# Reordering the three passes of the down products in a two-layer MoE kernel

## The chip, the cores and the metric

One Trainium2 chip, one core. The metric is the device time of one execution in microseconds; lower is better. The chip's engines are called as the profile calls them: PE (TensorE matmuls), PEld (TensorE weight loads), DVE (VectorE), ACT (ScalarE), POOL (GpSimd), SP (SyncE, which issues the transfers here).

## The reference

Attention with a memory term comes first, then two feed-forward layers over 2304 tokens (d_model 512, d_ff 2048). The two layers, cut to what matters here:

```python
def _moe_ref(x, w_in, w_out):
    h = x @ w_in
    g = np.maximum(0.01 * h, h)
    return (g @ w_out).astype(np.float32)

def _moe2_ref(x, w_in, w_out):
    h = x @ w_in
    g = h - np.tanh(h)
    return (g @ w_out).astype(np.float32)
```

`x @ w_in` is called up in the kernel, `g @ w_out` down.

## The kernel before

Each operand of the up and down products is split into a high part, rounded for one-pass matmuls, and a low part, the rest. A product is then three passes: high by high, high by low and low by high. The weights of both layers lie in SBUF as pairs `[high | low]` of 512 columns each; the activations as `gh` and `gl` (`xs[:, 0]` and `xs[:, 1]` for the input).

Tokens are cut into 9 blocks of 256, d_ff into 8 pairs of 128 columns (index `p`, with `s` for the two halves of a pair). For one block and one pair, an item below, the work is: 24 up matmuls (line 846) of 256 columns into one PSUM tile; the activation, which makes `g`; its high part `gh`, then its low part `gl`, which is `g - gh` and so comes after `gh`; and the down products, summed over all `p` in PSUM.

In layer 1 the down product has the weights as its stationary operand and `gh` or `gl` as its moving one: 24 matmuls of 256 columns (line 948) into `dn0` and `dn1`, each of which holds two of the four 128-row slices `m`. In layer 2 the activation is stationary and the weights move: 12 matmuls of 512 columns (line 1114) into two full tiles `dn[0]` and `dn[1]`, one for each half `t` of the tokens. The up matmuls of both layers, in `three()` (lines 843 to 849), run their three passes directly behind each other, with the same stationary tile in the first two.

The order of the work is set in two ways. Attention and layer 1 are put in order by a planner (`Schedule`, lines 86 to 221), which runs when the kernel is built: each piece of work has a cost in ns, what it reads and writes, and a priority. The planner goes forward in time; whenever an engine is free it gives it the first piece in order of priority whose inputs are there. Pieces of attention go ahead of pieces of layer 1 on PE (priority 0 against `MOE_PE` = 1), and the downs of item `p` (priority `2 * seq + 3`) go behind the ups of item `p+1` (`2 * (seq + 1)`). A down piece is two matmuls, at a cost of 240; an up piece is three, at 354. The result is one fixed order for each engine; on the chip an engine that waits for an input does not go on to what is behind it.

Layer 2 is ordered by hand (lines 1134 to 1152). Step `i` issues the ups of item `i`, its activation chain `act2` (inside which `act2_end` makes `gh` on ACT and `gl` on POOL for item `i-1`), and the downs of item `i - LAG2`, with `LAG2 = 2`. After the downs of a block's last item, `end2` copies `dn[0]` and then `dn[1]` out on ACT and stores them.

Of the kernel before, what the change touches and what calls it, by code (L numbers as in the profile page):

```python
# [9 lines left out]
F32 = mybir.dt.float32  # L10
# [213 lines left out]
MOE_PE = 1  # L224
# [18 lines left out]
def kernel(  # L243
# [14 lines left out]
    nc = tc.nc  # L258
    B, H, D, S = qkt.shape[0], qkt.shape[1], qkt.shape[2], qkt.shape[3] // 2
    DM, DFF = w1_in.shape  # L260
    KT = DM // 128
# [64 lines left out]
    for i in range(2):  # L326
        p = slice(64 * i, 64 * i + 64)
# [3 lines left out]
    wt = [[None] * NF for m in range(2)]  # L331
# [38 lines left out]
    p1 = ExitStack()  # L370
# [5 lines left out]
    dn_p = p1.enter_context(tc.tile_pool(name="dn", bufs=1, space=PSUM))  # L376
# [5 lines left out]
    sc = Schedule(RINGS)  # L382
    x_h = {}
    w_h = [[sc.new(None) for f in range(NF)] for m in range(2)]
# [468 lines left out]
    def layer1(n, p0, p1):  # L853

        kind, b = blocks[n]
        sop = lambda *a, **kw: sc.op(*a, prio=(-1, n), **kw)
        again = p0 > 0
        if again:

            halves = [sc.new("e0"), sc.new("e1")]  # L860

            def load_half(e, i):
                halves[i].tile = att.tile([128, 2, 256], F32, name=f"e{i}", bufs=1)
                nc.sync.dma_start(out=halves[i].tile, in_=xsv[n][:, 2 * i:2 * i + 2])

            for i in range(2):
                sop([("sp", 600)], lambda e, i=i: load_half(e, i), reads=[xv_h[n]], alloc=[halves[i]], lat=2600)
        elif kind == "R":
            x = sc.new("x")

            def load_x(e):
                x.tile = x_p.tile([128, KT, 256], F32, name="x")
                nc.sync.dma_start(out=x.tile, in_=x8s)

            sop([("sp", 600)], load_x, reads=[x8_h], alloc=[x], lat=2600)
        else:
            x = x_h[kind, b]
            if p1 < NP:

                def save_x(e):  # L880
                    nc.sync.dma_start(out=xsv[n], in_=x.tile)

                sop([("sp", 600)], save_x, reads=[x], writes=[xv_h[n]], lat=2600)
        xs = sc.new("xs")

        def x_half(i):
            return halves[i].tile if again else x.tile[:, 2 * i:2 * i + 2]

        def x_hi(e, i):
            if xs.tile is None:  # L890
                xs.tile = xs_p.tile([128, 2, KT, 256], F32R, name="xs")
            copy(e, xs.tile[:, 0, 2 * i:2 * i + 2], x_half(i))

        def x_lo(e, i):
            low(e, xs.tile[:, 1, 2 * i:2 * i + 2], x_half(i), xs.tile.bitcast(F32)[:, 0, 2 * i:2 * i + 2])

        for i in range(2):
            xi = halves[i] if again else x
            sop([("act", ACT(512)), ("dve", DVE(256))], lambda e, i=i: x_hi(e, i), reads=[xi] + [xs] * i,
                writes=[xs], alloc=[] if i else [xs])  # L900
            lo = sop([("dve", DVE(512))], lambda e, i=i: x_lo(e, i), reads=[xi, xs], writes=[xs])
            if again:
                att_ops.append(lo)
        dn = [sc.new("dn0"), sc.new("dn1")]
        last = None
        for p in range(p0, p1):
            seq = seqs[0]
            seqs[0] += 1
            ps = sc.new("up")

            def first_up(e, f, ps=ps):
                ps.tile = up_p.tile([128, 2, 256], F32, name="up")
                f()

            for s, kt, three in up_mms(lambda: xs.tile, lambda ps=ps: ps.tile, p):
                one = s == 0 and kt == 0
                sc.op(
                    [("pe", 354)], (lambda e, f=three, ff=first_up: ff(e, f)) if one else three,
                    reads=[xs, w_h[0][2 * p + s]] + ([] if one else [ps]), writes=[ps],
                    alloc=[ps] if one else [], prio=(MOE_PE, 2 * seq), order=one)  # L920
            g, gl, gh = sc.new("g"), sc.new("gl"), sc.new("gh")

            def leak(e, ps=ps, g=g):
                g.tile = g_p.tile([128, 512], F32, name="g")
                nc.scalar.activation(  # L925
                    out=g.tile, in_=ps.tile.rearrange("p a b -> p (a b)"), func=AF.Prelu, alpha=0.01)

            def g_hi(e, g=g, gh=gh):
                gh.tile = g_p.tile([128, 512], F32R, name="gh", bufs=RINGS["gh"])
                copy(e, gh.tile, g.tile)  # L930

            def g_lo(e, g=g, gh=gh, gl=gl):
                gl.tile = g_p.tile([128, 512], F32R, name="gl", bufs=RINGS["gl"])
                low(e, gl.tile, g.tile, gh.tile.bitcast(F32))

            sop([("act", ACT(512, True))], leak, reads=[ps], alloc=[g])
            sop(copies(512), g_hi, reads=[g], alloc=[gh])
            last = sop(lows(512), g_lo, reads=[g, gh], alloc=[gl])
            for j, (wh, gg) in enumerate(((0, gh), (1, gh), (0, gl))):
                for s in range(2):  # L940
                    for mm in range(0, KT, 2):

                        def down(e, p=p, j=j, wh=wh, gg=gg, s=s, mm=mm):
                            if p == p0 and j == 0 and s == 0:
                                dn[mm // 2].tile = dn_p.tile([128, 2, 256], F32, name=f"dn{mm // 2}")
                            w = wt[1][2 * p + s]
                            for m in (mm, mm + 1):
                                nc.tensor.matmul(  # L948
                                    dn[m // 2].tile[:, m % 2, :],
                                    lhsT=w[:, wh * 512 + m * 128:wh * 512 + (m + 1) * 128],  # L950
                                    rhs=gg.tile[:, s * 256:(s + 1) * 256],
                                    start=(p == p0 and s == 0 and m % 2 == 0 and j == 0),
                                    stop=(p == p1 - 1 and s == 1 and j == 2), skip_group_check=True)

                        begin = p == p0 and j == 0 and s == 0
                        d = dn[mm // 2]
                        sc.op([("pe", 240)], down, reads=[gg, w_h[1][2 * p + s]] + ([] if begin else [d]),
                              writes=[d], alloc=[d] if begin else [], prio=(MOE_PE, 2 * seq + 3))
        for i in range(2):
            x2 = sc.new("g")  # L960
            half = slice(2 * i, 2 * i + 2)

            def part_load(e, x2=x2, half=half):
                x2.tile = g_p.tile([128, 2, 256], F32, name="g")
                nc.sync.dma_start(out=x2.tile, in_=xps[n][:, half, :])

            def x2_out(e, i=i, x2=x2):
                if p0 > 0:
                    nc.vector.tensor_tensor(out=x2.tile, in0=dn[i].tile, in1=x2.tile, op=ALU.add)
                else:  # L970
                    x2.tile = g_p.tile([128, 2, 256], F32, name="g")
                    copy(e, x2.tile, dn[i].tile)

            def x2_store(e, x2=x2, half=half):
                nc.sync.dma_start(out=(x2s if p1 == NP else xps)[n][:, half, :], in_=x2.tile)

            if p0 > 0:
                sop([("sp", 500)], part_load, reads=[xp_h[n][i]], alloc=[x2], after=[last], lat=2300)
                sop([("dve", DVE(512))], x2_out, reads=[dn[i], x2], writes=[x2], port=False)
            else:  # L980
                sop(copies(512, True), x2_out, reads=[dn[i]], alloc=[x2], port=False)
            sop([("sp", 500)], x2_store, reads=[x2], writes=[x2_h[n] if p1 == NP else xp_h[n][i]], lat=2300)
# [57 lines left out]
    for p in range(NP):  # L1040
        for m in range(2):
            for f in (2 * p, 2 * p + 1):
                t = sc.new("v2")
# [60 lines left out]
    def down2(n, p):  # L1104
        if p == 0:
            state["dn"] = [dn2_p.tile([128, 512], F32, name=f"dn{i}") for i in range(2)]
        dn = state["dn"]
        gh, gl = state.pop((n, p))
        for j, (g, wh) in enumerate(((gh, 0), (gh, 1), (gl, 0))):
            for s in range(2):  # L1110
                w = wt[1][2 * p + s]
                for t in range(2):
                    c0 = s * 256 + t * 128
                    nc.tensor.matmul(  # L1114
                        dn[t], lhsT=g[:, c0:c0 + 128], rhs=w[:, wh * 512:(wh + 1) * 512],
                        start=(p == 0 and s == 0 and j == 0), stop=(p == NP - 1 and s == 1 and j == 2))
                    yield "pe"
# [16 lines left out]
    for i in range(len(items) + LAG2):  # L1134
        if i < len(items):
            n, p = items[i]
# [60 lines left out]
```

## Time and profile before

| | |
|---|---|
| median of 3 runs | 1082.89 us (1082.38 to 1083.25) |
| the profiled execution, whole | 1082.97 us |
| its span, first to last instruction | 1080.9 us |
| PE matmul busy | 1046.0 us, 97% |
| DVE busy | 754.3 us, 70% |
| ACT busy | 637.5 us, 59% |
| POOL busy | 104.0 us, 10% |
| mean granted TensorE clock | 0.988 of full speed |

The span leaves out about 2 us that lie around it. A matmul's own duration in the trace (about 285 ns for 256 columns) includes its way through the array, which overlaps with the next one's; what a matmul costs in a stream is the distance between starts. Rows that merge several instructions give the start of the first and the time they cover; in the chain of work that ended last the covered time is cut so that nothing is counted twice, and dividing it by the count gives the cost of one.

### The profile page before, as it was taken

Reading aid. Unit: us, or ns where it says so; the run is one execution under the profiler, and the core shown is the slowest. Engines: PE = TensorE matmul, PEld = TensorE weight load, DVE = VectorE, ACT = ScalarE, POOL = GpSimd, SP = SyncE. Lnnn points to the kernel's source line nnn. Section 1 sums busy time; section 2 is a strip of 40 time slices with the busy share of each in tenths; the row PEclk is TensorE's granted clock in tenths of the full one; section 3 lists DMA queues with packets and bytes.
Section 4 is the critical chain, followed back from the end, with each engine's and each line's share of the span. In section 5 each row is a group of like instructions: output and inputs, shape, how many; then the busy total and the mean of one; then the engine's idle time right before and its main releaser. Section 6 shows DMA issues by size and latency. Waiting matters only on the chain.

```text
span 1080.9 us, 20416 instructions
## 1 busy us (share of the span) xinstructions
PE 1046.0 (97%) x7488; PEld 921.3 (85%) x7488; DVE 754.3 (70%) x2044; ACT 637.5 (59%) x1357; POOL 104.0 (10%) x107
## 2 busy tenths in 40 slices
PE   5799999999999999999999999999999999999997
PEld 3567798787678977979999999999999999999996
DVE  6999999878766577664222267867777676777764
ACT  6899876667564266462111134766666666666664
POOL 1000000000000000000000000222222222221221
PEclk8699999999999999999999999999999999999999
DMA  7867754556554354243100056010101101010000
GB/s 231 261 178 219 232 173 119 158 144 166 158 147 135 114 159 140 91 124 124 40 2 21 1 156 196 1 40 1 40 1 39 40 1 40 1 40 20 1 20 20
DMA packets 116404, 102.53 MB, mean 95 GB/s; under 512 B 63824, under 2 KB 92496, under 8 KB 116304
## 3 DMA queue, kind: packets, MB, share of 16 engines
q1 hardware_dynamic: 116304, 101.23, 31.4%
q8 instruction: 59, 0.97, 0.4%
q14 instruction: 41, 0.34, 0.1%
HBM read 78.65 MB, written 22.54 MB: 94 GB/s over the span
## 4 chain that ended last, share of the span: by engine, by line
PE 77%; DVE 9%; DMA 6%; ACT 5%; issue 2%; SPq 1%; ACTq 0%; DVEq 0%
PE up L846 33%; PE dn L1114 18%; PE dn L948 14%; PE s L701 3%; PE s L582 3%; PE o L723 3%; DMA cv<-in_moe_w_out_dram 2%; DVE e L608 1%; PE o L668 1%; DVE cv L792 1%; DVE cv L797 1%; PE s L587 1%; ACT e L628 1%; DVE w L410 1%; DMA rq<-in_q_dram 1%
## 5 line engine op out<-in xcount | busy, mean ns | idle before, releaser
L846 PE MATMUL up<-xs,w 128*128 128x256 f32 x3456 | 454.4, 285 | 3.8 <-ACT g L925 2.4
L846 PEld LDWEIGHTS up<-xs,w 128*128 128x128 f32 x3456 | 435.2, 191 | 17.4 <-issue 6.2
L948 PE MATMUL dn<-gh,w 128*128 128x256 f32 x1152 | 161.1, 287 | 0.5 <-DVE gh L399 0.5
L948 PEld LDWEIGHTS dn<-gh,w 128*128 128x128 f32 x1152 | 146.5, 192 | 4.8 <-issue 3.6
L1114 PE MATMUL dn<-w,gh 128*128 128x512 f32 x576 | 145.3, 394 | 1.3 <-ACT gh L1101 1.3
L1091 DVE SCALAR_TENSOR_TENSOR gf<-u,w 128x512 f32<-128x512 f32 x72 | 86.2, 1197 | 82.3 <-ACT w L1088 82.3
L410 POOL TENSOR_TENSOR gl<-gf,gh 128x512 fp32r<-128x512 f32 x72 | 93.4, 1297 | 507.9 <-ACT gh L1101 504.4
L925 ACT ACTIVATE g<-up 128x512 f32<-128x512 f32 x72 | 42.7, 592 | 136.5 <-PE up L846 131.3
L1114 PEld LDWEIGHTS dn<-w,gh 128*128 128x128 f32 x576 | 103.0, 188 | 21.2 <-ACT gh L1101 2.0
L1083 ACT ACTIVATE u<-up 128x512 f32<-128x512 f32 x72 | 43.1, 598 | 123.8 <-PE up L846 123.8
L628 ACT ACTIVATE e<-e,mx 128x128 f32<-128x128 f32 (+4 forms) x144 | 82.7, 576 | 12.2 <-DVE mx L608 9.1
L948 PE MATMUL dn<-gl,w 128*128 128x256 f32 x576 | 85.0, 286 | 0.0
L948 PEld LDWEIGHTS dn<-gl,w 128*128 128x128 f32 x576 | 75.3, 192 | 3.2 <-issue 3.1
L1114 PE MATMUL dn<-w,gl 128*128 128x512 f32 x288 | 77.3, 390 | 0.0
L399 DVE CAST gh<-g 128x512 fp32r<-128x512 f32 x32 | 13.6, 426 | 87.6 <-ACT g L925 87.6
L608 DVE CUSTOM_DVE_ANT_0 e<-s,mask 128x128 f32<-128x128 f32 (+4 forms) x144 | 63.6, 481 | 12.3 <-PE s L582 6.5
L701 PE MATMUL s<-identr,e 128*128 128x128 f32 x448 | 64.7, 286 | 7.1 <-ACT e L645 5.2
L397 ACT ACTIVATE pt<-s 128x320 f32<-128x320 f32 (+4 forms) x145 | 56.4, 433 | 18.4 <-PE s L689 10.9
L701 PEld LDWEIGHTS s<-identr,e 128*128 128x128 f32 x448 | 51.1, 145 | 16.7 <-ACT e L645 7.4
L1114 PEld LDWEIGHTS dn<-w,gl 128*128 128x128 f32 x288 | 54.1, 188 | 12.1
L582 PE MATMUL s<-qk 64*128 64x256 f32 (+3 forms) x256 | 53.7, 497 | 9.7 <-DMA qk<-in_qkt_dram 7.0
L1085 DVE SCALAR_TENSOR_TENSOR hu<-up,u 128x512 f32<-128x512 f32 x72 | 49.6, 689 | 16.6 <-ACT u L1083 16.5
(100 smaller groups left out, 1329.4 us busy)
## 6 DMA issues: line engine op xcount, KB each, us to landing
w<-in_moe_w_in_dram SPq DMA_DIRECT2D x16, 512.0 KB, 5.0
w<-in_moe_w_out_dram SPq DMA_DIRECT2D x16, 512.0 KB, 5.6
cv<-in_moe_w_in_dram SPq DMA_DIRECT2D x32, 256.0 KB, 2.8
vs<-cv SPq DMA_DIRECT2D x64, 128.0 KB, 1.9
cv<-in_moe_w_out_dram SPq DMA_DIRECT2D x32, 256.0 KB, 2.9
v<-vs SPq DMA_DIRECT2D x32, 256.0 KB, 3.6
qk<-in_qkt_dram SPq DMA_DIRECT2D x16, 448.0 KB, 3.8
v<-in_v_dram SPq DMA_DIRECT2D x16, 320.0 KB, 3.4
```

The lines of the kernel that those rows point to most:

```text
L397: nc.scalar.activation(out=out, in_=in_, func=AF.Copy)
L410: (nc.vector if e == "dve" else nc.gpsimd).tensor_tensor(out=out, in0=in_, in1=high, op=ALU.subtract)
L582: nc.tensor.matmul(ss[j].tile[:, c0:c0 + nn], lhsT=qk.tile[p, a:a + 128], rhs=qk.tile[p, kc:kc + nn], start=True, stop=True)
L608: nc.vector.tensor_tensor_reduce(out=out, in0=in0, in1=in1, scale=-scale, scalar=mx.tile[:, 0:1] if t == 4 and j else BIG, op0=ALU.add, op ...
L628: nc.scalar.activation(out=x, in_=x, func=AF.Exp, scale=-1.0, bias=mx.tile[:, k:k + 1], accum_out=sm.tile[:, j:j + 1])
L701: nc.tensor.transpose(ss[j].tile[:, a:a + 128], x, ident)
L846: nc.tensor.matmul(ps()[:, s, :], lhsT=w[:, wh * 512 + kt * 128:wh * 512 + (kt + 1) * 128], rhs=xs()[:, xh, kt, :], start=(kt == 0 and j = ...
L948: nc.tensor.matmul(dn[m // 2].tile[:, m % 2, :], lhsT=w[:, wh * 512 + m * 128:wh * 512 + (m + 1) * 128], rhs=gg.tile[:, s * 256:(s + 1) * ...
L1083: nc.scalar.activation(out=u, in_=h, func=AF.Square)
L1085: nc.vector.scalar_tensor_tensor(out=hu, in0=h, scalar=c4, in1=u, op0=ALU.mult, op1=ALU.mult)
L1091: nc.vector.scalar_tensor_tensor(out=g, in0=u, scalar=lin, in1=w, op0=ALU.mult, op1=ALU.add)
L1114: nc.tensor.matmul(dn[t], lhsT=g[:, c0:c0 + 128], rhs=w[:, wh * 512:(wh + 1) * 512], start=(p == 0 and s == 0 and j == 0), stop=(p == NP - ...
```

## The change

In layer 1 the pieces of a down product become eight pieces of three matmuls, one for each half `s` and slice `m`; each runs the passes (high weights, `gh`), (high weights, `gl`), (low weights, `gh`) directly behind each other, costs 354 in the plan and reads both `gh` and `gl`. Before they were twelve pieces of two, which went through all of one pass before the next, and read `gh` or `gl`. In layer 2 the loop over the passes becomes the innermost: for each `s` and `t` the order is (`gh`, high weights), (`gh`, low weights), (`gl`, high weights). The number of matmuls is the same in both layers.

```diff
-            for j, (wh, gg) in enumerate(((0, gh), (1, gh), (0, gl))):
-                for s in range(2):
-                    for mm in range(0, KT, 2):
-
-                        def down(e, p=p, j=j, wh=wh, gg=gg, s=s, mm=mm):
-                            if p == p0 and j == 0 and s == 0:
-                                dn[mm // 2].tile = dn_p.tile([128, 2, 256], F32, name=f"dn{mm // 2}")
-                            w = wt[1][2 * p + s]
-                            for m in (mm, mm + 1):
-                                nc.tensor.matmul(
...
-                        sc.op([("pe", 240)], down, reads=[gg, w_h[1][2 * p + s]] + ([] if begin else [d]),
-                              writes=[d], alloc=[d] if begin else [], prio=(MOE_PE, 2 * seq + 3))
+            for s in range(2):
+                for m in range(KT):
+
+                    def down(e, p=p, gh=gh, gl=gl, s=s, m=m):
+                        if p == p0 and s == 0 and m % 2 == 0:
+                            dn[m // 2].tile = dn_p.tile([128, 2, 256], F32, name=f"dn{m // 2}")
+                        w = wt[1][2 * p + s]
+                        for j, (wh, gg) in enumerate(((0, gh), (0, gl), (1, gh))):
+                            nc.tensor.matmul(
...
+                    begin = p == p0 and s == 0 and m % 2 == 0
+                    d = dn[m // 2]
+                    sc.op([("pe", 354)], down, reads=[gh, gl, w_h[1][2 * p + s]] + ([] if begin else [d]),
+                          writes=[d], alloc=[d] if begin else [], prio=(MOE_PE, 2 * seq + 3))
...
-        for j, (g, wh) in enumerate(((gh, 0), (gh, 1), (gl, 0))):
-            for s in range(2):
-                w = wt[1][2 * p + s]
-                for t in range(2):
-                    c0 = s * 256 + t * 128
+        for s in range(2):
+            w = wt[1][2 * p + s]
+            for t in range(2):
+                c0 = s * 256 + t * 128
+                for j, (g, wh) in enumerate(((gh, 0), (gh, 1), (gl, 0))):
                     nc.tensor.matmul(
```

## Rows read from the trace of the kernel before

**Rows 1.** The page: busy time of PE, and the clock granted to it in 40 slices

```profile
PE 1046.0 (97%) x7488; PEld 921.3 (85%) x7488; DVE 754.3 (70%) x2044; ACT 637.5 (59%) x1357; POOL 104.0 (10%) x107
...
PEclk8699999999999999999999999999999999999999
```

**Rows 2.** Busy time in stretches: stretch, its length, then each engine, clock, DMA

```profile
0.00:60.00 60.00, 41.66 (x212) 28.18 (x213) 50.04 (x241) 45.53 (x135) 3.29 (x13) 0.80 0.80 238
60.00:500.00 440.00, 430.38 (x3297) 356.90 (x3297) 348.64 (x1321) 283.66 (x704) 7.28 (x22) 1.00 0.53 156
500.00:667.00 167.00, 167.00 (x1394) 167.00 (x1394) 62.11 (x112) 34.83 (x60) 0.00 (x0) 1.00 0.19 58
667.00:1075.00 408.00, 406.65 (x2592) 369.24 (x2590) 293.54 (x373) 272.36 (x458) 93.38 (x72) 1.00 0.07 24
```

**Rows 3.** The chain that ended last: start us, us, what; clean streams

```profile
358.76 2.88 PE up L846 x24
361.64 2.88 PE dn L948 x24
...
681.52 2.76 PE dn L1114 x12
```

**Rows 4.** The page's groups of instructions: the up matmuls and their weight loads

```profile
L846 PE MATMUL up<-xs,w 128*128 128x256 f32 x3456 | 454.4, 285 | 3.8 <-ACT g L925 2.4
L846 PEld LDWEIGHTS up<-xs,w 128*128 128x128 f32 x3456 | 435.2, 191 | 17.4 <-issue 6.2
```

**Rows 5.** Timeline of layer 2's first down product (start us, us, instructions)

```profile
674.93 0.63 ACT L1101 ACTIVATE gh<-gf 128x512 fp32r<-128x512 f32 x1 [0.61 <-DVE gf L1094]
...
675.61 2.12 PE L1114 MATMUL dn<-w,gh 128*128 128x512 f32 x8
675.64 1.29 POOL L410 TENSOR_TENSOR gl<-gf,gh 128x512 fp32r<-128x512 f32 x1 [203.39 <-ACT gh L1101]
...
677.57 1.07 PE L1114 MATMUL dn<-w,gl 128*128 128x512 f32 x4
```

**Rows 6.** Timeline of layer 2's last down product and the copies behind it

```profile
1071.58 0.63 ACT L1101 ACTIVATE gh<-gf 128x512 fp32r<-128x512 f32 x1 [2.47 <-DVE gf L1094]
1072.26 1.69 PEld L1114 LDWEIGHTS dn<-w,gh 128*128 128x128 f32 x8 [1.71 <-ACT gh L1101]
1072.26 2.12 PE L1114 MATMUL dn<-w,gh 128*128 128x512 f32 x8 [1.29 <-ACT gh L1101]
1072.28 1.29 POOL L410 TENSOR_TENSOR gl<-gf,gh 128x512 fp32r<-128x512 f32 x1 [3.51 <-ACT gh L1101]
...
1074.21 1.07 PE L1114 MATMUL dn<-w,gl 128*128 128x512 f32 x4
1075.09 1.09 ACT L1122 ACTIVATE ob<-dn 128x512 f32<-128x512 f32 x2 [2.88 <-PE dn L1114]
```

**Rows 7.** Timeline of layer 2 in its steady state

```profile
802.09 1.30 POOL L410 TENSOR_TENSOR gl<-gf,gh 128x512 fp32r<-128x512 f32 x1 [4.35 <-ACT gh L1101]
...
805.58 1.78 PE L1114 MATMUL dn<-w,gh 128*128 128x512 f32 x7
```

**Rows 8.** The instructions of line 948: durations in ns, first and last start

```profile
L948 PEld LDWEIGHTS dn<-gh,w x1152: 186/192/249, 60.2 to 665.6; 128*128 128x128 f32 x192
```

**Rows 9.** Timeline of layer 1 at two of its 72 down products

```profile
205.01 0.69 DVE L410 TENSOR_TENSOR gl<-g,gh 128x512 fp32r<-128x512 f32 x1 [0.39 <-ACT gh L397]
205.03 1.25 PEld L948 LDWEIGHTS dn<-gh,w 128*128 128x128 f32 x10 [0.25 <-ACT gh L397]
...
350.14 1.29 DVE L410 TENSOR_TENSOR gl<-g,gh 128x512 fp32r<-128x512 f32 x2
...
350.25 1.55 PE L948 MATMUL dn<-gh,w 128*128 128x256 f32 x11 [0.47 <-DVE gh L399]
```

More of the change, by code (lines that the diff above doesn't have):

```diff
@@ L938, in layer1 @@
             last = sop(lows(512), g_lo, reads=[g, gh], alloc=[gl])
-            for j, (wh, gg) in enumerate(((0, gh), (1, gh), (0, gl))):
-                for s in range(2):
-                    for mm in range(0, KT, 2):
-                        def down(e, p=p, j=j, wh=wh, gg=gg, s=s, mm=mm):
-                            if p == p0 and j == 0 and s == 0:
-                                dn[mm // 2].tile = dn_p.tile([128, 2, 256], F32, name=f"dn{mm // 2}")
-                            w = wt[1][2 * p + s]
-                            for m in (mm, mm + 1):
-                                nc.tensor.matmul(
[L949 to L956, printed above, removed]
-                        sc.op([("pe", 240)], down, reads=[gg, w_h[1][2 * p + s]] + ([] if begin else [d]),
-                              writes=[d], alloc=[d] if begin else [], prio=(MOE_PE, 2 * seq + 3))
@@ new lines, in layer1 @@
+            for s in range(2):
[6 more added lines that the diff above has]
+                            nc.tensor.matmul(
+                                dn[m // 2].tile[:, m % 2, :],
+                                lhsT=w[:, wh * 512 + m * 128:wh * 512 + (m + 1) * 128],
+                                rhs=gg.tile[:, s * 256:(s + 1) * 256],
+                                start=(p == p0 and s == 0 and m % 2 == 0 and j == 0),
+                                stop=(p == p1 - 1 and s == 1 and j == 2), skip_group_check=True)
+                    begin = p == p0 and s == 0 and m % 2 == 0
+                    d = dn[m // 2]
+                    sc.op([("pe", 354)], down, reads=[gh, gl, w_h[1][2 * p + s]] + ([] if begin else [d]),
+                          writes=[d], alloc=[d] if begin else [], prio=(MOE_PE, 2 * seq + 3))
```

## The prediction

> **What bounds the kernel now.** I read the page's busy times first: PE is busy for 1046.0 of 1080.9 us, no other engine comes near, and from the third of the 40 slices on the granted clock is at 9 tenths or more [rows 1]. Then the same by stretch, to see where PE is not busy [rows 2]. In the first 60 us it idles 18.3 us, while inputs arrive. From 60 to 500 us, where attention and layer 1 share it, it idles 9.6 us, at a granted clock of 1.00, the level of 2.4 GHz, as in all that follows. From 500 to 667 us, layer 1 alone, it never idles. From 667 to 1075 us, layer 2, it idles 1.35 us. So the time is the sum of PE's streams and of the few holes in them. The change can act through three things only: what a matmul costs in its stream, new holes where a matmul now waits for something, and the plan of the stretch from 60 to 500 us.
>
> **What a matmul costs in the new order.** The new order puts two matmuls with the same stationary tile side by side. The up product has that order already, and the down product of layer 1 has it nowhere. In the chain of work a clean stream of ups takes 2.88 us for 24, and a clean stream of downs takes 2.88 us for 24: 120 ns each, with and without the neighbour [rows 3]. The load isn't left out for the second of two equal ones either: 3456 loads stand beside 3456 up matmuls [rows 4]. So for the 1728 matmuls of layer 1, I put the reordering at 0.
>
> In layer 2 the matmul has 512 columns, and no row shows one behind another with the same stationary tile. One costs 2.76 / 12 = 230 ns [rows 3]. Twice the cost of an up would be 240 ns, so 230 ns holds a part of about 2 x 120 - 230 = 10 ns that doesn't grow with the columns (230 = a + 512 b and 120 = a + 256 b, thus a = 10). If equal neighbours saved all of that, the bound below is 288 x 10 ns = -2.9 us. On the other side, three matmuls in a row now add into one PSUM tile, where before two tiles took turns; the up product adds 12 in a row into one place at the same 120 ns as the downs that take turns, so this is 0 too, and the bound above, again 10 ns on two thirds of 864, is +5.8 us. The nearest row, the up stream with both features at once, says 0; I take 0.
>
> A rule speaks for a gain here. The Trainium skill, "TensorE: Matmul & The Clock Gate", section "Step-by-step: what each phase is for", says that a load is an instruction of its own so that one load can serve many matmuls. The counts of loads above say that this kernel's way of issuing matmuls doesn't use that; by the rule one load in three would go, by the rows none.
>
> **The wait for gl.** Before, the third pass alone read `gl`, from matmul 9 of 12 on in layer 2 and from 17 of 24 on in layer 1. Now the third matmul (layer 2) or the second (layer 1) does. What stands behind it on PE is the rest of the down product, then the next ups, so a late `gl` holds all of PE.
>
> In the steady state of layer 2, `gl` is done at 802.09 + 1.30 = 803.39 us for a down product that starts at 805.58 us: 2.2 us early, plus two matmuls [rows 7]. So the 70 products between pay nothing. The first and the last one do.
>
> First product: `gh` ends at 675.56 us. The eight `gh` matmuls end with the start of the gl matmuls at 677.57, so at 230 ns each they begin in effect at 677.57 - 1.84 = 675.73 us, 0.17 behind `gh`. The third matmul is due at 675.73 + 0.46 = 676.19 us. POOL's `gl` runs from 675.64 to 676.93 us; with the same 0.17 behind it the third matmul starts at 677.10 us [rows 5]. Before, five more matmuls hid that. PE loses **+0.91 us**, and as PE is then busy until the end, nothing takes it back.
>
> Last product: `gh` ends at 1072.21 us, the matmuls begin in effect at 1074.21 - 1.84 = 1072.37, the third is due at 1072.83. `gl` ends at 1073.57 us, so the third starts at 1073.73 us [rows 6]: **+0.90 us**.
>
> In return `dn[0]` is complete three matmuls before the end, not one. Before, ACT's two copies take 1.09 us from 1075.09 us on, so the second starts at 1075.64 us, while the last matmul ended at 1074.21 + 1.07 = 1075.28 us [rows 6]: it stood behind the first copy for 0.36 us. Now the first copy is done by then, and the second starts 0.04 us after the last matmul, which is what the first copy took after its own (1075.28 - 0.23 = 1075.05 us). That is **-0.32 us**. Layer 2 in all: 0.91 + 0.90 - 0.32 = **+1.5 us**.
>
> The bound on these two stalls from below is 0, if PE could take later `gh` matmuls past a waiting one. The same page of the Trainium skill, same section, says that only weight loads are pulled ahead and that matmuls keep their order, which speaks against the change; no row here tests it, since at both places nothing else was queued that could have run.
>
> **Layer 1: gl and the plan.** Nothing differs before the first down matmul at 60.2 us [rows 8], so the 18.3 idle us of the start stay. In the stretch of layer 1 alone the downs of an item follow the ups of the next, 2.88 us, and `gl` is ready; PE stays full there: 0. Between 60 and 500 us, four of the 72 products began before their `gl` was done. The two worst: at 205.03 us with `gl` ending at 205.70 (0.67 late), and at 350.25 us with `gl`, the first of two in 1.29 us, ending near 350.83 (0.58 late); before both PE had already stood idle for `gh` [rows 9]. In the old order these would be stalls of 1.25 us together. The planner knows of the new wait and gives PE other work if any is ready. With 0 (always other work) and 1.25 us (never) as the ends I take the middle, **+0.6 us**.
>
> The plan itself comes out new, since pieces, costs and readiness differ. A down piece is planned at 118 ns a matmul in place of 120, a true 120 in the chain: under 0.05 us an item, nothing. A piece of attention now waits for up to three matmuls, 0.36 us, in place of 0.24 us, but PE works meanwhile; and there are at most 8 places in a product where attention can cut in, in place of 12, so PE changes less often between the two. What a new order is worth can't be read from the old one. Its bound on the side of a gain is the 9.6 idle us [rows 2]; on the side of a loss I take as much again. The row nearest to it is the 9.6 us themselves, the holes that this planner leaves in such a stretch; another order from the same rules should leave about as many: 0.
>
> **The sum.** 1.5 + 0.6 + 0 = +2.1 us. The profiled execution took 1082.97 us, against a median of 1082.89 us, the same to 0.01%; with the median, 1082.89 + 2.1 = **1085.0 us**.
>
> **The rivals.** 0.2%, about what a measurement of this kernel can tell from no change, is 2.2 us, so the forecast stands just at that edge.
>
> First, the forecast's mechanism: two stalls in layer 2, little in layer 1, 1083.2 to 1087.0 us. Chance 0.60. About half of it lies above 1085.06.
>
> Second, **the new plan fills holes**: fewer cuts let PE run attention in longer stretches, and half of the 9.6 us goes. For it speaks that pieces of attention cut layer 1 often there; against it, that the named idle time has many small releasers and no single one that the change touches. 1085.0 - 4.8 = 1080.2 us. It decides the sign from 2.1 us of filled holes on. Chance 0.10.
>
> Third, **the new plan opens holes**: `gl` is on DVE behind its other work, and DVE is busy for 348.6 of 440 us there [rows 2]. If a third of what the plan leaves idle comes on top, 3.2 us, it is 1088.2 us; with half, 1089.8 us. Chance 0.20.
>
> Fourth, **equal neighbours are cheaper in layer 2**: 220 in place of 230 ns for one in three, -2.9 us, so 1082.1 us; the rule on loads quoted above would be its reason. The ups speak against it. Chance 0.05. That the reordering does nothing at all, the stalls included because PE passes the waiting matmul, is 1082.9 us, chance 0.05.
>
> **How the numbers follow.** Slower by over 0.2%: half of the first (0.30) and 0.85 of the third (0.17), 0.47. Faster: 0.8 of the second (0.08), and a sliver of the fourth, 0.09. The rest, 0.44, is within 0.2%. The range reaches up into the third rival and down past the fourth: 1081.0 to 1089.5 us leaves out about 0.1 on the lower side and 0.1 on the upper. The likeliest case alone has 1083.2 to 1087.0 us.
>
> **What the profile after would show.** The matmul count of lines 846 and of both downs the same, loads as many as matmuls; 12 of layer 2's downs in 2.76 us and 24 of layer 1's in 2.88 us. In the timeline of the first and last product of layer 2, two `gh` matmuls, then a hole of about 0.9 us that ends with POOL's `gl`, and ACT's second output copy right behind the last matmul. Between 60 and 500 us PE's idle time near 10 us. The prediction is wrong if the streams' cost per matmul moves by some ns (1 ns on 864 matmuls is 0.9 us), or if PE's idle time from 60 to 500 us moves by more than about 3 us.

## The result and the profile after

The change made the kernel slower: 1092.3 us against 1083.14 us, medians of six runs each, ratio 1.0074 with a 95% interval of 1.0056 to 1.0092. That is +8.0 us (+6.1 to +10.0); the forecast was +2.1 us, and its range ended at 1089.5 us. The ratio is taken over all runs and isn't the quotient of the medians, which differ by 9.2 us; every change in us below is a ratio less 1, times the time of the kernel before.

The page of the kernel after, as [rows 1], and the busy time by stretch, as [rows 2] (the last stretch, at the same 667 to 1075 us, holds another part of the work by now, so layer 2 is read from the timelines below):

```profile
PE 1052.1 (96%) x7488; PEld 922.5 (85%) x7488; DVE 752.3 (69%) x2044; ACT 636.9 (58%) x1358; POOL 103.4 (9%) x106
...
PEclk8799999999999999999999999999999999999999
...
L846 PEld LDWEIGHTS up<-xs,w 128*128 128x128 f32 x3456 | 435.9, 191 | 17.8 <-issue 8.3
L948 PEld LDWEIGHTS dn<-gh,w 128*128 128x128 f32 x1152 | 188.2, 192 | 5.6 <-issue 5.2
```

```profile
0.00:60.00 60.00, 40.53 (x204) 26.66 (x205) 49.46 (x228) 44.94 (x133) 3.27 (x13) 0.83 0.80 237
60.00:500.00 440.00, 428.69 (x3238) 351.82 (x3238) 346.73 (x1335) 281.91 (x707) 6.81 (x21) 0.99 0.54 154
500.00:667.00 167.00, 167.00 (x1394) 167.00 (x1393) 57.33 (x102) 33.77 (x55) 0.00 (x0) 1.00 0.18 55
667.00:1075.00 408.00, 407.36 (x2627) 371.33 (x2626) 294.86 (x377) 271.51 (x456) 90.78 (x70) 1.00 0.08 27
```

What to see: there are still 7488 weight loads for 7488 matmuls. In layer 1 alone, PE runs the same 1394 matmuls in 167 us as before [rows 2]. The difference is in the stretch from 60 to 500 us. There the busy time falls by only 1.7 us, from 430.38 to 428.69, and this hides most of the loss: the count beside it falls from 3297 to 3238 matmuls, and 59 at 120 ns are 7.1 us. The first 60 us lack another 8. The loss is all in the first 100 us of that stretch, here before and then after:

```profile
60.00:160.00 100.00, 97.57 (x756) 80.81 (x756) 99.80 (x394) 87.38 (x232) 4.02 (x7) 1.00 0.69 207
```

```profile
60.00:160.00 100.00, 93.72 (x683) 74.61 (x683) 98.07 (x406) 83.21 (x227) 4.67 (x7) 0.97 0.69 202
```

From 160 to 500 us the kernel after does 13 matmuls more (2557 against 2544). By line of code, attention gets about as many in these 100 us as before, 311 against 306. Layer 1, which fills what attention leaves free, gets 372 in place of 450; these 78 at 120 ns are 9.4 us. DVE is as full there as PE, 99.80 of 100 us before, which the average of 348.6 in 440 us in the prediction doesn't show.

A PE whose matmuls run slower, or that waits for less than the 0.3 us for which a matmul is shown, looks full in this view; the count beside it gives it away. Layer 2's first down product starts at 683.62 us (below), 8.0 us after that of [rows 5].

Layer 2's first and last down product in the timeline after, to be held against [rows 5] and [rows 6]:

```profile
682.93 0.63 ACT L1101 ACTIVATE gh<-gf 128x512 fp32r<-128x512 f32 x1 [0.60 <-DVE gf L1094]
...
683.62 0.73 PE L1114 MATMUL dn<-w,gh 128*128 128x512 f32 x2
683.64 1.28 POOL L410 TENSOR_TENSOR gl<-gf,gh 128x512 fp32r<-128x512 f32 x1 [205.24 <-ACT gh L1101]
...
684.97 0.50 PE L1114 MATMUL dn<-w,gl 128*128 128x512 f32 x1 [0.62 <-POOL gl L410]
...
685.31 0.62 PE L1114 MATMUL dn<-w,gh 128*128 128x512 f32 x2
```

```profile
1080.49 0.63 ACT L1101 ACTIVATE gh<-gf 128x512 fp32r<-128x512 f32 x1 [2.48 <-DVE gf L1094]
...
1081.20 1.27 POOL L410 TENSOR_TENSOR gl<-gf,gh 128x512 fp32r<-128x512 f32 x1 [3.52 <-ACT gh L1101]
...
1082.52 0.50 PE L1114 MATMUL dn<-w,gl 128*128 128x512 f32 x1 [0.62 <-POOL gl L410]
...
1082.86 0.62 PE L1114 MATMUL dn<-w,gh 128*128 128x512 f32 x2
...
1084.45 1.28 ACT L1122 ACTIVATE ob<-dn 128x512 f32<-128x512 f32 x2 [3.33 <-PE dn L1114]
...
1084.70 0.39 PE L1114 MATMUL dn<-w,gl 128*128 128x512 f32 x1
```

In both, two `gh` matmuls run and PE then waits for POOL's `gl`. In the first, `gh` ends at 683.56, so the third matmul was due at 683.56 + 0.17 + 0.46 = 684.19; the fourth starts at 685.31, the third thus in effect at 685.08: 0.89 us late (forecast 0.91). In the last one it is 1082.63 in place of 1081.75: 0.88 us (forecast 0.90). From the last matmul's end to the end of the span it is now 1090.3 - 1085.09 = 5.2 us, before 1080.9 - 1075.28 = 5.6 us: -0.4 us (forecast -0.32). In the steady state an item takes what it took:

```profile
800.31 3.04 PE L846 MATMUL up<-xs,w 128*128 128x256 f32 x24
805.96 3.04 PE L846 MATMUL up<-xs,w 128*128 128x256 f32 x24
```

5.65 us from one item's ups to the next, and 24 x 0.12 + 2.76 us, the price of [rows 3], is 5.64 us. The chain of work that ended last of layer 1 alone shows the 24 downs in 2.88 us again:

```profile
502.17 2.88 PE dn L948 x24
505.05 2.88 PE up L846 x24
```

So the loss is in the stretch that the planner puts in order. PE's waits there between 60 and 160 us, longest in total first (us, times, longest), before and then after:

```profile
PE s L545 <- DVE ph L528: 1.5, 1, 1.5
PE s L582 <- ACT pt L397: 0.4, 1, 0.4
PE o L668 <- DVE pT L399: 0.3, 1, 0.3
```

```profile
PE o L668 <- ACT pT L397: 2.0, 2, 1.8
PE s L587 <- DVE mx L608: 1.8, 1, 1.8
PE s L545 <- POOL ph L528: 1.5, 1, 1.5
```

With two short ones it is 5.9 us, before it was 2.2 us. None of them is for `gl`; from 60 to 500 us PE waits for that once, 0.3 us:

```profile
PE dn L948 <- DVE gl L410: 0.3, 1, 0.3
```

They are attention's own waits, at places where the planned order has nothing else for PE to do. One place in the timeline, with all engines, and then in that of PE alone:

```profile
75.91 0.90 POOL L528 TENSOR_TENSOR ph<-ph,dn 128x256 f32<-128x256 f32 x1 [20.62 <-DVE dn L521]
...
76.86 0.44 PE L545 MATMUL s<-identr,ph 128*128 128x128 f32 x2 [1.47 <-POOL ph L528]
```

```profile
79.12 1.13 PE L668 MATMUL o<-pT,mb 128*128 128x256 f32 x2 [1.81 <-ACT pT L397]
```

The plan gave the division of `ph` to POOL, and PE's transposes and the matmul behind them wait for it, then for ACT's copy of `pT`. Behind this, and again around 143 us, the granted clock falls, where before it was 1.00; by stretch (the clock is the last number but two):

```profile
70.00:80.00 10.00, 6.67 (x45) 4.55 (x43) 10.00 (x48) 8.04 (x25) 0.90 (x1) 0.96 0.74 214
80.00:90.00 10.00, 9.45 (x62) 6.64 (x63) 10.00 (x51) 9.02 (x26) 0.00 (x0) 0.87 0.82 260
140.00:150.00 10.00, 8.15 (x50) 6.83 (x49) 9.22 (x24) 5.92 (x13) 1.41 (x2) 0.83 0.75 253
```

At half speed for a share of these stretches, 0.04 + 0.13 + 0.17 of 10 us and twice that in time, 6.8 us run at 1.2 GHz and cost up to 3.4 us of work. With 1.7 us more of idle time from 60 to 500 us and about 1 us in the first 60 us, that is, as an estimate, some 6 of the 8 us; the rest is in delays too short for these views, and I couldn't place it.

### The profile page after: what moved, and what is told of

Its sections match the earlier page's. It is cut to its first block, busy times and chain, and to the rows that moved or that the text cites. A ratio compares the mean times of both kernels' runs of the same rounds, so it can differ in the third digit from the quotient of the medians.

```text
span 1090.3 us, 20392 instructions
## 1 busy us (share of the span) xinstructions
PE 1052.1 (96%) x7488; PEld 922.5 (85%) x7488; DVE 752.3 (69%) x2044; ACT 636.9 (58%) x1358; POOL 103.4 (9%) x106
## 4 chain that ended last, share of the span: by engine, by line
PE 45%; issue 29%; POOL 8%; DVE 7%; DMA 5%; ACT 4%; SPq 1%; POOLq 0%; ACTq 0%; DVEq 0%
PE dn L948 16%; PE up L846 16%; POOL gl L410 8%; PE o L723 3%; PE s L582 3%; PE s L701 3%; DMA cv<-in_moe_w_in_dram 2%; PE o L668 1%; PE s L587 1%; DMA rq<-in_q_dram 1%; DVE cv L792 1%; ACT e L628 1%; DVE e L608 1%; PE s L545 1%; DMA cv<-in_moe_w_out_dram 1%
## 5 line engine op out<-in xcount | busy, mean ns | idle before, releaser
L948 PE MATMUL dn<-gh,w 128*128 128x256 f32 x1152 | 232.0, 287 | 0.0
L948 PEld LDWEIGHTS dn<-gh,w 128*128 128x128 f32 x1152 | 188.2, 192 | 5.6 <-issue 5.2
L1114 PE MATMUL dn<-w,gh 128*128 128x512 f32 x576 | 179.2, 392 | 0.9 <-ACT gh L1101 0.9
L948 PE MATMUL dn<-gl,w 128*128 128x256 f32 x576 | 163.2, 283 | 0.4 <-DVE gl L410 0.3
L1114 PE MATMUL dn<-w,gl 128*128 128x512 f32 x288 | 113.8, 395 | 1.4 <-POOL gl L410 1.2
L948 PEld LDWEIGHTS dn<-gl,w 128*128 128x128 f32 x576 | 110.4, 192 | 1.3 <-DVE gl L410 1.0
L608 DVE CUSTOM_DVE_ANT_0 e<-s,mask 128x128 f32<-128x128 f32 (+4 forms) x144 | 63.5, 481 | 10.3 <-PE s L582 7.3
L784 DVE TENSOR_SCALAR cv<-cv 128x256 f32<-128x256 f32 (+1 forms) x96 | 31.6, 332 | 43.3 <-ACT cv L781 40.1
```

The source lines that it names most:

```text
L608: nc.vector.tensor_tensor_reduce(out=out, in0=in0, in1=in1, scale=-scale, scalar=mx.tile[:, 0:1] if t == 4 and j else BIG, op0=ALU.add, op ...
L948: nc.tensor.matmul(dn[m // 2].tile[:, m % 2, :], lhsT=w[:, wh * 512 + m * 128:wh * 512 + (m + 1) * 128], rhs=gg.tile[:, s * 256:(s + 1) * ...
L1114: nc.tensor.matmul(dn[t], lhsT=g[:, c0:c0 + 128], rhs=w[:, wh * 512:(wh + 1) * 512], start=(p == 0 and s == 0 and j == 0), stop=(p == NP - ...
```

## The experiments

Five theories were held against each other, all on layer 1: **1**, the early read of `gl`, or the order of the passes, costs the time; **2**, the coarser pieces cost it; **3**, any change of what the planner reads gives another order, whose worth is chance; **4**, a plan that takes the down products for shorter than they are costs it; **5**, being wrong on them in either direction costs it, the more the further. All kernels compute the whole reference. Each was run against the kernel before in the same session; the before medians were 1082.51 to 1083.78 us.

**Layer 2 alone, and layer 1 alone.** The diff above, one half of it at a time.

> Layer 1 as before, layer 2 with the new order. The two stalls at its ends and the earlier output copy are all that layer 2 pays: 1.0 to 1.8 us over the kernel before, with the attention stretch unchanged to within 1 us. A rival that has layer 2's matmuls cost more in the new order would give over 3 us here; the profile after already has them at 230 ns.

Measured: ratio 1.0020 (1.0006 to 1.0035), +2.2 us (+0.7 to +3.8). This holds the forecast's +1.5 us and doesn't give layer 2 any of the missing 6.

> Layer 1 with the new order, layer 2 as before. All theories of layer 1: about 8 us over the kernel before (the last down product of layer 1 came 8.05 us later in the profile after), less if the slow start of that profile was chance (0.9 us). Under 4 us would mean that layer 2 delays more than its own trace shows.

Measured: ratio 1.0053 (1.0034 to 1.0072), +5.7 us (+3.7 to +7.8). That is less than the 8 us that all theories of layer 1 had, but with layer 2's +2.2 us it adds up to the whole change. The cause of the miss is in layer 1. The same stretches, in the profile of this kernel:

```profile
60.00:160.00 100.00, 93.72 (x683) 74.58 (x682) 98.04 (x393) 83.55 (x227) 4.67 (x7) 0.97 0.69 204
160.00:500.00 340.00, 335.73 (x2576) 279.08 (x2575) 248.66 (x930) 198.88 (x481) 2.14 (x14) 1.00 0.50 142
```

**The wait for gl, and the piece size, each by itself.** The first is the kernel before with one edit:

```diff
-                        sc.op([("pe", 240)], down, reads=[gg, w_h[1][2 * p + s]] + ([] if begin else [d]),
+                        sc.op([("pe", 240)], down, reads=[gh, gl, w_h[1][2 * p + s]] + ([] if begin else [d]),
```

> Layer 1 in the old order, pieces of two matmuls at a cost of 240, but every piece reads gl as well in the plan, so that the plan starts no down product before gl. Layer 2 as before. Theory 1, the early wait for gl costs the time: about +6 to +9 us. Theory 2, the coarser pieces cost it: within 2 us of before. Theory 3, any change of what the planner reads gives another order that is worth some us either way: anywhere from -5 to +10 us, without regard to the kind of change.

Measured: ratio 0.9977 (0.9964 to 0.9990), -2.5 us. Theory 1 falls as far as the wait goes. The second cuts the old order of passes in threes:

```diff
+            mms = [(j, wh, gg, s, m) for j, (wh, gg) in enumerate(((0, gh), (1, gh), (0, gl))) for s in range(2) for m in range(KT)]
+            for k in range(0, 24, 3):
+                piece = mms[k:k + 3]
...
+                sc.op([("pe", 354)], down, reads=gs + ws + [d for d in ds if d not in new],
+                      writes=ds, alloc=new, prio=(MOE_PE, 2 * seq + 3))
```

> Layer 1 in the old order of passes, cut into eight pieces of three at a cost of 354, so that the first five pieces read gh alone as before. Layer 2 as before. Theory 1 (wait for gl): within 2 us of before. Theory 2 (coarser pieces): +6 to +9 us. Theory 3 (another order, of whatever worth): anywhere from -5 to +10 us.

Measured: ratio 1.0080 (1.0057 to 1.0102), +8.7 us. That fitted theory 2, and theory 3 as well.

**Order, cut and cost apart.** The new order in pieces of two, with the code of the cut above, and of one; the changed layer 1 with 360, and the kernel before with 236 for the cost of a piece:

```diff
+            mms = [(j, wh, gg, s, m) for s in range(2) for m in range(KT) for j, (wh, gg) in enumerate(((0, gh), (0, gl), (1, gh)))]
+            for k in range(0, 24, 2):
...
-                    sc.op([("pe", 354)], down, reads=[gh, gl, w_h[1][2 * p + s]] + ([] if begin else [d]),
+                        sc.op([("pe", 120)], down, reads=[gg, w_h[1][2 * p + s]] + ([] if begin else [d]),
...
-                        sc.op([("pe", 240)], down, reads=[gg, w_h[1][2 * p + s]] + ([] if begin else [d]),
+                        sc.op([("pe", 236)], down, reads=[gg, w_h[1][2 * p + s]] + ([] if begin else [d]),
```

```diff
-                    sc.op([("pe", 354)], down, reads=[gh, gl, w_h[1][2 * p + s]] + ([] if begin else [d]),
+                    sc.op([("pe", 360)], down, reads=[gh, gl, w_h[1][2 * p + s]] + ([] if begin else [d]),
```

> Layer 1 in the new order of passes, but cut into twelve pieces of two at a cost of 240, as the old order was. Layer 2 as before. Theory 2 (coarser pieces cost the time, the order of the passes costs nothing): within 3 us of the kernel before. Theory 1 (the order of the passes): +5 to +9 us. Theory 3 (any other plan, of whatever worth): anywhere from -5 to +10 us.

Measured: ratio 0.9996 (0.9978 to 1.0014). The new order of passes costs nothing by itself.

> Layer 1 in the new order of passes, cut into 24 pieces of one matmul at a cost of 120. Layer 2 as before. Theory 2: no slower than the kernel before, within 3 us or faster, since attention can cut in at more places. Theory 1: +5 to +9 us. Theory 3: anywhere from -5 to +10 us.

Measured: ratio 1.0075 (1.0056 to 1.0094), +8.1 us. Finer pieces aren't safer, which theory 2 had them be.

> Layer 1 of the changed kernel, pieces of three, planned at a cost of 360 in place of 354, so at the 120 ns a matmul that the chain shows. Layer 2 as before. Theory 2: still +4 to +9 us. Theory 3: anywhere from -5 to +10 us. A further theory 4, that the plan's too small cost did it: within 2 us of before.

Measured: ratio 0.9992 (0.9976 to 1.0008). The same order of passes, pieces, waits and matmuls as in layer 1 of the changed kernel, and 6.6 us faster than with 354 (-0.9 against +5.7 us). Theory 2 falls here.

> The kernel before with one number changed: a down piece of layer 1 is planned at a cost of 236 in place of 240 (354 for three, per matmul), which gives another order of the same pieces. Theory 2: within 3 us of before. Theory 3: anywhere from -5 to +10 us. Theory 4 (the too small cost): +5 us or more.

Measured: ratio 1.0041 (1.0026 to 1.0055), +4.4 us, for one number in the plan of the kernel before. Theory 3, or 4, a little below its +5 us.

**Costs on both sides.** The same number again: 362 and 358 in the changed layer 1, 360 in the pieces of three in the old order, 244 in the kernel before.

> Layer 1 of the changed kernel, planned at 362 for a piece of three (120.7 ns a matmul). Layer 2 as before. Theory 4, a plan whose down products are too cheap costs the time: within 3 us of before, like the one with 360. Theory 3, each order is worth what chance gives it: anywhere from -5 to +10 us, without regard to 360 beside it.

Measured: ratio 0.9972 (0.9956 to 0.9988), -3.0 us.

> The same, planned at 358 (119.3 ns a matmul). Theory 4: between those with 354 and 360, so 0 to +4 us over before. Theory 3: anywhere from -5 to +10 us.

Measured: ratio 0.9982 (0.9970 to 0.9993), -2.0 us. Theory 4 had 0 to +4 us.

> Old order of passes, pieces of three, planned at 360 in place of 354. Layer 2 as before. Theory 4: within 3 us of before, where 354 gave +8.7 us. Theory 2, coarser pieces: +5 to +10 us again. Theory 3: anywhere from -5 to +10 us.

Measured: ratio 0.9979 (0.9964 to 0.9993), -2.3 us, where 354 gave +8.7 us. Theory 2 falls a second time.

> The kernel before, with a down piece planned at 244 in place of 240 (122 ns a matmul). Theory 4, in which only a too small cost hurts: within 3 us of before. Theory 3: anywhere from -5 to +10 us; over +3 us speaks for it, since this is as far from 120 as the +3.4 us at 118, on the other side.

Measured: ratio 1.0074 (1.0053 to 1.0095), +8.0 us. Theory 4 alone doesn't cover this; theories 3 and 5 do. (The +3.4 us that this expectation and a later one give for 236 is about the difference of the medians, 3.3 us; by the ratio it is +4.4 us.)

The same stretch in three profiles shows what the time goes with: before_cost244, then after_cost362, then after_cost352 (below), each from 60 to 160 us.

```profile
60.00:160.00 100.00, 93.89 (x683) 74.72 (x680) 95.77 (x397) 82.51 (x225) 3.36 (x6) 0.95 0.66 200
```

```profile
60.00:160.00 100.00, 96.77 (x728) 78.97 (x727) 96.74 (x394) 82.76 (x226) 3.03 (x6) 0.97 0.70 207
```

```profile
60.00:160.00 100.00, 93.21 (x678) 73.61 (x677) 96.64 (x396) 84.61 (x229) 1.82 (x4) 0.95 0.69 202
160.00:500.00 340.00, 329.87 (x2483) 273.60 (x2483) 245.72 (x916) 200.20 (x478) 3.30 (x15) 0.98 0.48 136
```

These slow plans get 683 and 678 matmuls into these 100 us, the fast one 728. The order of the kernel before got 756 in its own profile and 732 in that of the kernel with layer 2 alone (last section), so 728 is within what one order does from run to run; 683, which the changed layer 1 has in both its profiles, didn't come up with it. After_cost352 loses a second time, from 160 us on: 2483 matmuls where the changed layer 1 alone has 2576. And a slow plan need not lose before 160 us at all: single_new has

```profile
60.00:160.00 100.00, 96.32 (x740) 78.88 (x738) 97.95 (x396) 87.75 (x237) 5.62 (x9) 1.00 0.70 207
160.00:500.00 340.00, 328.77 (x2478) 270.10 (x2477) 251.33 (x935) 194.18 (x468) 2.30 (x14) 0.98 0.48 136
```

What the slow plans share is PE's idle time from 60 to 500 us. In one profile of each plan in the table below it is 10.6 to 16.9 us for the seven that are over 4 us slower, and 6.0 to 9.6 us for the eleven others; the order of the kernel before has 10.3 us in the profile with layer 2 alone, so the groups all but touch. It is only a part of what they lose: the changed layer 1 alone has 0.9 us more of it than the kernel before, and takes 5.7 us more.

At the place of the timeline above, 73 to 80 us, after_cost362 has `ph` on DVE, and PE waits 0.18 us in place of 1.47, and 0.78 in place of 1.81:

```profile
74.70 0.41 PE L545 MATMUL s<-identr,ph 128*128 128x128 f32 x2 [0.18 <-DVE ph L528]
75.89 0.70 PE L668 MATMUL o<-pT,mb 128*128 128x256 f32 x2 [0.78 <-ACT pT L397]
```

Having `ph` on DVE doesn't rule out such holes: this kernel and the one before have one each behind it, 1.1 and 1.5 us, a little later in the same stretch.

**A smooth cost against chance.** Two more costs of the changed layer 1, one more of the kernel before, and the fine cut at 121.

> Changed kernel's layer 1 at 366 for three (122 ns a matmul), layer 2 as before. Theory 5, being wrong on the true 120 ns costs smoothly: +5 to +8 us, as the old pieces at 122. Theory 3, chance: anywhere from -5 to +10 us, and within 2 us of before or faster speaks for it.

Measured: ratio 0.9981 (0.9964 to 0.9998), -2.1 us. Theory 5 falls: as far from the true 120 ns as 244 for two, and not slow.

> The same at 352 (117.3 ns a matmul). Theory 5: +6 to +10 us, at least as slow as with 354. Theory 3: anywhere from -5 to +10 us; under +3 us speaks for it.

Measured: ratio 1.0129 (1.0101 to 1.0157), +14.0 us, the slowest of all.

> The kernel before with 238 for a piece of two (119 ns a matmul). Theory 5: between the 0 of 240 and the +3.4 us of 236, so 0 to +3 us. Theory 3: anywhere from -5 to +10 us; over +4 us or under -2 us speaks for it.

Measured: ratio 0.9995 (0.9977 to 1.0012).

> Pieces of one matmul in the new order, planned at 121 in place of 120. Theory 5, with a further cost of so fine a cut: +6 to +10 us as with 120. Theory 3: anywhere from -5 to +10 us; under +4 us speaks for it.

Measured: ratio 0.9995 (0.9978 to 1.0012), where 120 gave +8.1 us: 1 ns in the plan of a piece is worth some 8 us.

**The ups' cost in place of the downs'.** Line 918 has it; the second kernel has 366 there, with the downs at 354 as changed.

```diff
-                    [("pe", 354)], (lambda e, f=three, ff=first_up: ff(e, f)) if one else three,
+                    [("pe", 348)], (lambda e, f=three, ff=first_up: ff(e, f)) if one else three,
...
-                    sc.op([("pe", 354)], down, reads=[gh, gl, w_h[1][2 * p + s]] + ([] if begin else [d]),
+                    sc.op([("pe", 360)], down, reads=[gh, gl, w_h[1][2 * p + s]] + ([] if begin else [d]),
```

> Changed kernel's layer 1 with ups planned at 348 and downs at 360 for three, so that an item of 48 matmuls is planned at 5664 ns, as in the changed kernel, where the chip takes 5760. Layer 2 as before. Theory 4, an item planned too short costs the time: +4 to +9 us. Theory 3, chance: like the most of the other plans, within 3 us of before or faster.

Measured: ratio 1.0031 (1.0015 to 1.0046), +3.4 us, just outside what either theory gave.

> Ups planned at 366 and downs at 354 as in the changed kernel, an item thus at 5760 ns, the true length. Layer 2 as before. Theory 4: within 3 us of before or faster, where the changed layer 1 alone was +5.8 us. If it is the downs' own cost that counts, or chance that this cut at 354 is a bad order: +4 to +9 us.

Measured: ratio 1.0085 (1.0068 to 1.0101), +9.2 us. The planned length of the item isn't the cause; theory 4, as put there, falls. The other reading in that expectation, that the downs' own cost counts, stays as a rival of chance: it would cover the plans at 118 ns and less, but not the slow ones at 120 and 122 ns.

All plans by the cost of one down matmul, in us against before:

| planned ns | pieces and order | change, us |
|---|---|---|
| 117.3 | three, new (352) | +14.0 |
| 118 | three, new (354) | +5.7 |
| 118 | three, new, ups 366 | +9.2 |
| 118 | three, old | +8.7 |
| 118 | two, old (236) | +4.4 |
| 119 | two, old (238) | -0.5 |
| 119.3 | three, new (358) | -2.0 |
| 120 | two, old: before | 0 |
| 120 | two, old, reads gl | -2.5 |
| 120 | two, new | -0.4 |
| 120 | one, new | +8.1 |
| 120 | three, new (360) | -0.9 |
| 120 | three, new, ups 348 | +3.4 |
| 120 | three, old | -2.3 |
| 120.7 | three, new (362) | -3.0 |
| 121 | one, new | -0.5 |
| 122 | three, new (366) | -2.1 |
| 122 | two, old (244) | +8.0 |

Shown: with the same matmuls, the order that the plan gives is worth anything from -3 to +14 us. The five plans at 118 ns and less are all slow, and of the thirteen at 119 and more three are. That is a pattern and no cause: the test of the item's length went against it, and what in a plan makes the costly order is open. That in layer 1 the neighbours with equal weights have no part in it is shown by the rows with the new order that aren't slower than before.

## Why the prediction was wrong

**Streams: right.** 24 downs of layer 1 take 2.88 us with equal neighbours too, an item of layer 2 takes 5.65 us as before, and loads stand one to one beside matmuls. So the rule on loads that the prediction takes from the Trainium skill does nothing in this kernel as it issues its matmuls; a third of the loads gone, as it would be by that rule, isn't what the trace shows.

**Stalls of layer 2: right.** 0.89, 0.88 and -0.4 us against 0.91, 0.90 and -0.32. The wait for POOL's `gl` with `gh` matmuls queued behind it is at the same time the test that was missing before: PE didn't pass the waiting matmul, as the Trainium skill, "TensorE: Matmul & The Clock Gate", section "Step-by-step: what each phase is for", has it; the trace agrees, with 0.62 us of idle time before it in both products.

**gl in layer 1, +0.6 us: within its bounds of 0 and 1.25.** PE waits for `gl` for 0.3 us from 60 to 500 us. The -2.5 us with the wait alone in the plan is no price of the wait, since that plan is another order as well.

**The plan, 0: the step that failed.** "Another order from the same rules should leave about as many" holes: it measured +5.7 us with layer 1 alone. The step took PE's idle time as the measure of what a plan costs, and by the prediction's own sign, a move of over 3 us in it, nothing was wrong: it moved by 1.7 us, from 9.6 to 11.3. The rest went where idle time doesn't show it: up to 3.4 us to the lower clock, and a part that isn't placed. The bound beside it, 9.6 us more, was the right size (plans at up to +9.2 us, one at +14.0), but the range was cut at 1089.5 us by giving this case a chance of 0.20. And the sentence before it, that a piece planned at 118 ns in place of 120 is worth nothing, weighed the 48 ns an item by which the plan is off, not the other order that follows from it; with 360 in place of 354 the changed layer 1 is no slower than before. The rival that came nearest is the third, more holes, priced at 3.2 to 4.8 us on top. Its reason, `gl` late behind DVE's other work, is not what the trace shows: but for 0.3 us, the waits are for `ph`, `pT`, `mx` and other tiles of attention.

**A version that beats both:** the new order of layer 1 planned at 362, with the old layer 2, is 3.0 us faster than before (0.12 to 0.44%). It is the best of eighteen plans, so a part of that may be the luck of the pick. What it shows is the plan, not the order of passes.

## What to carry to other kernels

Where a planner builds the order of the work, an edit of a piece is also a draw of a new order; price that draw from other draws (one cost moved by 1 to 3%, the work left alone) before giving the edit itself any of the difference. A read of a late operand that moves to the front of a product costs its lead only where the product has no slack, at the first and the last item of a pipeline here; both can be worked out to a few hundredths of a us from the timeline. When a stretch gets slower, compare the number of instructions done in it, not only the busy time.

## What the runs showed of the hardware

Runs of one and the same order of work differ by the granted clock. The kernel with layer 2 alone has layer 1's order from before, and the same hole at 76 to 79 us that PE has there before; but in its profile the clock fell behind it, and stayed at 1.00 in that of the kernel before. The stretches of the kernel before, then those of the kernel with layer 2 alone:

```profile
60.00:80.00 20.00, 17.77 (x139) 13.56 (x139) 20.00 (x103) 18.91 (x58) 1.23 (x2) 1.00 0.64 176
80.00:90.00 10.00, 10.00 (x81) 8.34 (x78) 10.00 (x47) 9.94 (x31) 0.00 (x0) 1.00 0.81 233
```

```profile
60.00:80.00 20.00, 17.77 (x138) 13.55 (x137) 20.00 (x105) 18.64 (x57) 1.24 (x2) 0.99 0.64 174
80.00:90.00 10.00, 10.00 (x57) 7.52 (x57) 7.74 (x39) 7.38 (x24) 0.00 (x0) 0.67 0.75 203
```

57 matmuls in 10 us at a clock of 0.67 against 81 at 1.00, with PE busy for the same 17.77 of the 20 us ahead of it. The kernel before itself ran from 1078.86 to 1088.28 us in 25 runs beside the second set of experiments, at mean clocks from 0.991 down to 0.983, the lower mostly in the longer runs. A hole that PE gets away with in one run costs it some 3 us in the next (24 matmuls at 120 ns), so one profile of each kernel isn't enough to read a difference of 3 us from this stretch.
